# Retention with two mixtures: signs of weight conversions on ScalarE, sums and splits at other queue places

## The chip, the cores and the metric

The kernel runs on one core of a Trainium2 chip. Its time is the device time of one execution in microseconds (us), and the median of several executions is compared. Five engines work side by side, each through its own queue, in order: TensorE (PE in the profile, its weight loads PEld), VectorE (DVE), ScalarE (ACT), GpSimd (POOL) and SyncE (SP, here only issuing DMA transfers). An instruction waits at the head of its queue until what it needs is there, and everything behind it waits too.

## The reference

Three stages follow one another. First a retention layer over two sequences of 768 tokens and 8 heads of 64, in blocks of 64 tokens with a state that is carried on and decays by `lam` per head:

```python
intra = np.einsum('bhij,bhjd->bhid', np.einsum('bhic,bhjc->bhij', qb, kb) * Dmask[None], vb)
inter = np.einsum('bhid,bhde->bhie', qb * lam_pow[None], kv_state)
out[:, :, sl] = intra + inter
kv_state = lam_block[None, :, None, None] * kv_state + np.einsum('bhsd,bhse->bhde', kb_dec, vb)
```

Its output, 1536 tokens by 512, goes through a layer with 2048 hidden units, `relu(x @ w_in)**2 @ w_out`, and then through one with 1536 hidden units:

```python
gate = 1.0 / (1.0 + np.exp(-(x @ w_gate)))
val = x @ w_val
return (gate * val @ w_out).astype(np.float32)
```

The weights of both layers arrive in float64; `w_gate` is large (scaled by 45.7).

## The kernel before

**Weights.** The program reads a weight unit (128 x 512 numbers) as pairs of 32-bit words (`raw`) and makes fp32 from the bits. There are 68 such conversions: 32 units of the first layer (`w1`) and 36 of the second (`w2`: gate, val and output unit for each of 12 blocks of 128 hidden units). `conv_act` is the part on ScalarE: `j` from the high words (L155), and `r` from the low words. It has two forms. With `sign=False`, `r` is one operation (L163). With `sign=True`, ScalarE writes `r` in two 16-bit halves: the lower from the low words (L159), the upper, with sign, from the high words (L161). `conv_dve` is the part on VectorE: a shift of `j` (L186, or L196 for the units whose sign is turned over), then L189, which merges the sign, and the addition (L181). With `sign=True` L189 is left out. Before the change 16 conversions, all in the first layer, use that form. The result is stored in DRAM and read back when it is used.

**Splits.** Every fp32 matrix enters TensorE as a sum of a high part (cast to fp32r on ScalarE: `whi`, `xch`, `ah`, `gh`, `gq`, `wq`) and a low part (difference on VectorE: `wlo`, `xcl`, `al`, `gl`). Each product is three matmuls: high by high, high by low, low by high. The names in the profile are these tiles, `p` is a PSUM bank.

**The second layer.** From 311 to 407 us TensorE works on the first 512 tokens, block by block (`step_2`): `stage_a` (L472) makes gate and val of block f, `stage_b` (L486) the output part of block f-1. In between, `elem` makes `g` (sigmoid `r` on ScalarE at L507, product on VectorE at L508) and `split_g` makes `gh` (L516) and `gl` (L518). For block f+1, `split_w` makes three `whi` (L458) and three `wlo` (L460). The other 1024 tokens go by Strassen's scheme: `combine_x` prepares the seven token combinations (`t` at L577 and L583, casts `xch` at L561, `xcl` at L564) while the first 512 tokens are in work. From 407 to 527 us `strassen` multiplies with the gate and val weights, a key (two blocks, gate or val) after the other; per key seven products A11, S1, S2, S4, S3, A12, A22 (`block`, L678). `snap` copies a bank to SBUF on ScalarE (`s`, L687) before a later product may add into the bank; `total` (`c`, L692) adds on VectorE. Gate results go through the sigmoid at L792, val results are multiplied with it (L796). Then `later` makes the four sums `gs` (L813), which with `g` are the seven operands of the output product; `by_unit` splits them into `gq` high (L859) and low (L862). From 527 us to the end `blocks_out` (L995) multiplies them with seven combinations of output weights, in two passes q of the six blocks. The weight combinations `ws` come from `sum_out_w` (four VectorE operations at L924 for each of six block pairs, one load `wr` before and four stores after). `prepare_w` loads them (`bring`, into the two places D and `rows` in turn), casts `wq` (L948) and subtracts (L952).

**What sets the order.** All of it is recorded by one program that walks along TensorE's instructions with a model clock. `at(pos, fn)` puts work on an agenda; when `passed` moves the clock past `pos`, the agenda's `fn` is recorded there, on whichever engines it uses. `T3`, `T4`, `T5` and `T6` are model times at which the second layer, its Strassen part, the output passes and the second of these begin. The queue order of each engine is thus fixed when the program is built, and the times in the agenda are model times, not measured ones.

Of the kernel before, what the change touches and what calls it, by code (L numbers as in the profile page):

```python
# [7 lines left out]
F32 = mybir.dt.float32  # L8
F32R = mybir.dt.float32r
AF = mybir.ActivationFunctionType  # L10
# [28 lines left out]
def retention_moe_kernel(  # L39
# [24 lines left out]
    nc = tc.nc  # L64
# [25 lines left out]
    clock = [0.0]  # L90
    agenda = []

    def at(pos, fn):
        agenda.append((pos, len(agenda), fn))
# [47 lines left out]

    ready = []

    def conv_act(more=True, sign=False):

        if not to_conv or to_conv[0] not in raw_t:
            return  # L150
        key = to_conv.pop(0)
        t = raw_t.pop(key)
        j = unit("j")
        r = unit("r", I32)
        nc.scalar.activation(j, t[:, :, 1].bitcast(F32), AF.Copy, scale=2.0**-112)  # L155
        low = t[:, :, 0].bitcast(mybir.dt.uint32)
        if sign:
            parts = r.bitcast(mybir.dt.int16).rearrange("p (n two) -> p n two", two=2)
            nc.scalar.activation(parts[:, :, 0], low, AF.Copy, scale=2.0**-29)  # L159
            top = parts[:, :, 1].bitcast(mybir.dt.float16)  # L160
            nc.scalar.activation(top, t[:, :, 1].bitcast(F32), AF.Copy, scale=2.0**-60)  # L161
        else:
            nc.scalar.activation(r, low, AF.Copy, scale=2.0**-29)  # L163
        ready.append((key, j.bitcast(I32), r, sign))
        if more:
            load_w(1)

    def conv_dve():

        if not ready:  # L170
            return []
        key, j, r, sign = ready.pop(0)
        ph, f, u = key
        flip = ph == 2 and u < 2 and f % 2 == 0
        m = unit("m", I32)
        w = unit("u")
        if ph == 1:
            w_t[key] = w

        def last():  # L180
            nc.vector.tensor_tensor(out=w.bitcast(I32), in0=m, in1=r, op=ALU.add)  # L181
            n_stored[0] += 1
            at(clock[0] + 4.0, lambda: nc.sync.dma_start(out=w32[ph][f, u], in_=w))

        ops = [
            lambda: nc.vector.tensor_scalar(  # L186
                out=m, in0=j, scalar1=3, scalar2=None, op0=ALU.logical_shift_left
            ),
            lambda: nc.vector.scalar_tensor_tensor(  # L189
                out=m, in0=j, scalar=-(2**31), in1=m, op0=ALU.bitwise_and,  # L190
                op1=ALU.bitwise_xor if flip else ALU.bitwise_or,
            ),
            last,
        ]
        if flip:
            ops[0] = lambda: nc.vector.tensor_scalar(  # L196
                out=m, in0=j, scalar1=3, scalar2=-(2**31),
                op0=ALU.logical_shift_left, op1=ALU.bitwise_or,
            )
        if sign:  # L200
            assert not flip
            ops.pop(1)
        return ops

# [582 lines left out]
    def pair_in_2(i):  # L787
        gate = {}

        def use_gate(di, t, c, in_psum):  # L790
            r = gate[di, t] = unit("r")
            nc.scalar.activation(r, c, AF.Sigmoid)  # L792

        def use_val(di, t, c, in_psum):
            g = unit("g")
            nc.vector.tensor_tensor(out=g, in0=c, in1=gate.pop((di, t)), op=ALU.mult)  # L796
            n = GB.get((di, t))
            raw[n] = g
            if n is not None:
                done(n)  # L800
            if n == 5:
                later()

        raw = {}

        def done(n):
            if i in VIA_DRAM:
                g = raw[n]
                at(clock[0] + 2.5, lambda: nc.sync.dma_start(out=gs_dram[i, :, n], in_=g))

        def total(n, a, b, op):
            raw[n] = unit("gs")
            nc.vector.tensor_tensor(out=raw[n], in0=raw[a], in1=raw[b], op=op)  # L813
            done(n)

        def later():


            t = clock[0] + (7.5 if i == 5 else 0.0)
            at(t + 1.5, lambda: total(0, None, 6, ALU.add))  # L820
            at(t + 3.5, lambda: total(1, 0, 4, ALU.subtract))
            at(t + 5.5, lambda: total(2, 4, None, ALU.subtract))
            at(t + 7.5, lambda: total(3, 5, 1, ALU.subtract))
            if i in VIA_DRAM:
                at(t + 7.5, raw.clear)
            elif i == 0:
                at(t + 7.5, lambda: by_unit(i, dict(raw), clock[0], 4.5))
            else:
                at(t + 7.5, lambda: by_unit(i, dict(raw), T5 + 16.5, 0.8))

        return [use_gate, use_val]
# [22 lines left out]
    def by_unit(i, raw, pos, gap):  # L854

        def hi(n):
            if i not in gq:
                new_set(i)
            nc.scalar.copy(block_of(gq[i][0], n), raw[n])  # L859

        def lo(n):
            nc.vector.tensor_tensor(  # L862
                out=block_of(gq[i][1], n), in0=raw.pop(n), in1=block_of(gq[i][0], n),
                op=ALU.subtract,
            )

        for k, n in enumerate((4, 5, 1, 0, 2, 3, 6)):
            at(pos + gap * k, lambda n=n: hi(n))
            at(pos + gap * k + 1.2, lambda n=n: lo(n))
# [96 lines left out]
    def blocks_out():  # L966


        for q in range(2):
            acc, v = {}, {}  # L970

            def put(name, t, e, cols=slice(0, TB), eng=nc.sync):
                col = (t + 1) * TB
                eng.dma_start(
                    out=out[2 * q + e, :, col + cols.start : col + cols.stop],
                    in_=v[name][:, cols],
                )

            def add(name, k, other, cols=slice(0, TB)):
                if name not in v:  # L980
# [162 lines left out]
        stage_b(*prev.pop())  # L1143
        evacuate(ph)

    def convert(pos):
        at(pos, conv_act)
        at(pos + 2.0, lambda: run(conv_dve()))


# [2 lines left out]
    T3 = T2 + 24 * NF1 * MM  # L1153
    T4 = T3 + (36 * NF2 - 12) * MM
    T5 = T4 + (12 + 42 * NF2) * MM

    with tc.manual_schedule():
# [95 lines left out]
        for f in range(2, NF2):  # L1253
            at(T3 + (36 * (f - 1) - 12) * MM - 8.0, lambda f=f: load_units(2, f))
        for k in range(3 * NF2 - n_out):
            convert(T3 + 2.0 + 3.6 * k)
        for i in range(NF2 // 2):
            sum_out_w(i, T4 - 64.0 + 9.0 * i)
        keys = [(2, i, u) for i in range(NF2 // 2) for u in range(2)]
        prepare_a(keys[0], T4)  # L1260
        at(T4 - 28.0, lambda: combine_a((2, 0, 1)))
# [2 lines left out]
        for f in range(NF2):  # L1264
            step_2(f)
        T6 = T5 + 6 * STEP
        by_unit_through_dram(1, T5 - 14.0, T5 - 7.0)
        through_dram(2, T5 - 4.0, T5 + 1.5)
        through_dram(3, T5 + 1.0, T5 + 6.5)
        through_dram(4, T5 + 6.0, T5 + 11.5)  # L1270
        for n, load, pos in (
            (0, -21.0, -13.0), (1, -12.0, -1.5), (2, -6.0, 4.0),
            (3, 1.0, 8.8), (4, 6.0, 13.5), (5, 11.0, 18.3),
        ):
            prepare_w(0, n, n, T5 + load, T5 + pos)
        for n, i, load, pos in (
            (0, 5, -12.5, -5.0), (1, 4, -7.5, -1.0), (2, 3, -3.0, 3.5),
            (3, 0, 1.0, 8.0), (4, 2, 6.0, 12.5), (5, 1, 10.0, 15.5),
        ):
            prepare_w(1, n, i, T6 + load, T6 + pos)  # L1280
        by_unit_through_dram(2, T6 - 7.0, T6 + 5.0)
# [68 lines left out]
```

## Time and profile before

| | us |
|---|---|
| runs, lowest, median, highest | 589.77, 589.95, 595.18 |
| profiled execution | 591.19 |
| its span in the trace | 589.4 |
| PE busy | 576.1 (98%) |
| DVE busy | 474.0 (80%) |
| ACT busy | 366.9 (62%) |

The span is the time from the first to the last instruction in the trace of one execution, and the execution's own time is 1.8 us longer. Busy time is the time in which an engine worked on at least one instruction. TensorE's granted clock is 1.00 of its full rate in all stretches shown. Records of matmuls overlap: a new one may start every 0.227 us, and the record of one lasts 0.39. In the timelines a number in brackets is the idle time just before an instruction, and behind the arrow stands what ended it.

### The profile page before, as it was taken

The numbers are of one execution on the slowest core, as the hardware profiler recorded it, in microseconds if no ns is written. First come the engines' busy times: TensorE is split into PE (matmuls) and PEld (weight loads), VectorE is DVE, ScalarE is ACT, GpSimd is POOL, SyncE is SP. The second block draws the span as 40 slices with busy tenths as digits, with TensorE's granted clock in tenths as the row PEclk, the third lists the DMA queues.
The fourth block names the chain that finished last, engine by engine and source line by source line (L and its number), as shares of the span: only waits on it lengthen the run. The fifth ranks groups of instructions, "written<-read, shape, count | busy, mean of one in ns | idle before, by whom it ended". The sixth has DMA issues, their size and how long they took to land.

```text
span 589.4 us, 9045 instructions
## 1 busy us (share of the span) xinstructions
PE 576.1 (98%) x3172; PEld 471.7 (80%) x3172; DVE 474.0 (80%) x732; ACT 366.9 (62%) x605; POOL 47.6 (8%) x48
## 2 busy tenths in 40 slices
PE   9899999999999999999999999999999999999996
PEld 8788888767888888888888887888887888878885
DVE  2789896899788868988777788985678877789974
ACT  4679999997656557756467645544545554475470
POOL 1751100000000000000000000022012110000000
PEclk9999999999999999999999999999999999999999
DMA  7999896783253297999978878994547678488681
GB/s 260 413 405 376 311 310 216 226 293 105 71 189 134 108 304 263 413 408 413 404 273 289 307 246 272 339 305 102 174 89 205 187 229 233 153 320 307 205 304 72
DMA packets 69008, 150.83 MB, mean 256 GB/s; under 512 B 7137, under 2 KB 14305, under 8 KB 68962
## 3 DMA queue, kind: packets, MB, share of 16 engines
q1 hardware_dynamic: 64656, 144.34, 68.8%
q0 software_dynamic: 3360, 3.93, 4.5%
q10 hardware_dynamic: 946, 1.97, 1.0%
q8 instruction: 25, 0.41, 0.3%
q14 instruction: 21, 0.17, 0.1%
HBM read 106.43 MB, written 42.21 MB: 252 GB/s over the span
## 4 chain that ended last, share of the span: by engine, by line
PE 80%; DVE 9%; ACT 4%; DMA 3%; issue 3%; POOL 0%; DVEq 0%; SPq 0%; ACTq 0%
PE p L678 28%; PE p L1066 15%; PE p L472 15%; PE p L486 10%; PE p L995 8%; DMA gr<-gs 2%; PE p L315 2%; PE p L400 2%; DMA decay<-w_dram 1%; DVE at L350 1%; PE p L383 1%; DVE m L189 1%; PE p L411 1%; DVE gq L862 1%; DVE xcl L564 1%
## 5 line engine op out<-in xcount | busy, mean ns | idle before, releaser
L678 PE MATMUL p<-xch,ah 128*128 128x512 f32 x280 | 110.0, 393 | 1.0 <-ACT s L687 0.5
L678 PE MATMUL p<-xcl,ah 128*128 128x512 f32 x280 | 109.1, 390 | 0.0
L678 PE MATMUL p<-xch,al 128*128 128x512 f32 x280 | 109.1, 390 | 0.0
L678 PEld LDWEIGHTS p<-xch,ah 128*128 128x128 f32 x280 | 52.6, 188 | 15.3 <-ACT s L687 3.5
L687 ACT COPY s<-p 128x512 f32<-128x512 f32 x60 | 35.2, 588 | 43.8 <-PE p L678 43.7
L678 PEld LDWEIGHTS p<-xch,al 128*128 128x128 f32 x280 | 52.6, 188 | 11.0
L678 PEld LDWEIGHTS p<-xcl,ah 128*128 128x128 f32 x280 | 52.6, 188 | 10.6
L995 PE MATMUL p<-gq,wq 128*128 128x512 f32 x252 | 57.7, 390 | 1.0 <-DVE wq L952 1.0
L692 DVE TENSOR_TENSOR c<-p,s 128x512 f32<-128x512 f32 x60 | 41.2, 687 | 19.4 <-PE p L678 19.0
L995 PEld LDWEIGHTS p<-gq,wq 128*128 128x128 f32 x252 | 47.2, 188 | 11.4 <-DVE wq L952 1.6
L155 ACT ACTIVATE j<-raw 128x512 f32<-128x512 f32 x68 | 45.7, 672 | 12.9 <-issue 5.3
L181 DVE CUSTOM_DVE_ANT_0 u<-m,r 128x1024 uint16<-128x1024 uint16 x68 | 49.6, 729 | 4.7 <-ACT r L161 1.7
L460 DVE TENSOR_TENSOR wlo<-u,whi 128x512 fp32r<-128x512 f32 x68 | 46.0, 708 | 6.2 <-ACT whi L458 5.0
L1066 PE MATMUL p<-g2h,whi 128*128 128x512 f32 x128 | 49.8, 389 | 0.0
L1066 PE MATMUL p<-g2l,whi 128*128 128x512 f32 x128 | 49.8, 389 | 0.0
L1066 PE MATMUL p<-g2h,wlo 128*128 128x512 f32 x128 | 49.8, 389 | 0.0
L472 PE MATMUL p<-xh,wlo 128*128 128x512 f32 x160 | 43.8, 395 | 3.8 <-DVE wlo L460 3.8
L472 PE MATMUL p<-xh,whi 128*128 128x512 f32 x160 | 43.2, 392 | 0.0
L472 PE MATMUL p<-xl,whi 128*128 128x512 f32 x160 | 42.8, 390 | 0.0
L163 ACT ACTIVATE r<-raw 128x512 int32<-128x512 uint32 x52 | 34.5, 663 | 8.2 <-PE p L1066 4.9
L472 PEld LDWEIGHTS p<-xh,wlo 128*128 128x128 f32 x160 | 29.4, 188 | 12.6 <-DVE wlo L460 6.9
L458 ACT CAST whi<-u 128x512 fp32r<-128x512 f32 x68 | 37.9, 615 | 0.5 <-PE p L472 0.5
(129 smaller groups left out, 1048.3 us busy)
## 6 DMA issues: line engine op xcount, KB each, us to landing
raw<-in_w SPq DMA_DIRECT2D x68, 512.0 KB, 6.4
w<-u SPq DMA_DIRECT2D x68, 256.0 KB, 5.1
u<-w SPq DMA_DIRECT2D x52, 256.0 KB, 5.1
a<-w SPq DMA_DIRECT2D x20, 512.0 KB, 4.1
g<-g SPq DMA_DIRECT2D x32, 256.0 KB, 4.4
g<-g SPq DMA_DIRECT2D x16, 512.0 KB, 7.6
gr<-gs SPq DMA_DIRECT2D x24, 256.0 KB, 5.6
kv<-in_kv SPq DMA_DIRECT2D x11, 512.0 KB, 10.4
```

The costliest lines, as they stand in the source:

```text
L155: nc.scalar.activation(j, t[:, :, 1].bitcast(F32), AF.Copy, scale=2.0**-112)
L163: nc.scalar.activation(r, low, AF.Copy, scale=2.0**-29)
L181: nc.vector.tensor_tensor(out=w.bitcast(I32), in0=m, in1=r, op=ALU.add)
L458: nc.scalar.copy(hi, src)
L460: lambda lo=lo, src=src, hi=hi: nc.vector.tensor_tensor(out=lo, in0=src, in1=hi, op=ALU.subtract)
L472: nc.tensor.matmul(acc, lhsT=a[:, kk * P : (kk + 1) * P], rhs=b[:, kk, :], start=i == 0, stop=i == 11,)
L486: nc.tensor.matmul(acc[e], lhsT=a[:, e * P : (e + 1) * P], rhs=b, start=first and i == 0, stop=last and i == 2,)
L678: nc.tensor.matmul(acc, lhsT=w[:, col, kk * P : (kk + 1) * P], rhs=x[:, kk, :], start=start and i == 0, stop=stop and i == 5, skip_group_c ...
L687: nc.scalar.copy(s, acc)
L692: nc.vector.tensor_tensor(out=c, in0=acc, in1=s, op=ALU.add)
L995: nc.tensor.matmul(acc[k], lhsT=a[:, wn], rhs=block_of(b, gn), start=first and n == 0, stop=last and n == 3 * len(group) - 1,)
L1066: nc.tensor.matmul(acc[e, t], lhsT=a[:, e * P : (e + 1) * P], rhs=b[:, t, :], start=first and i == 0, stop=last and i == 2,)
```

## The change

Four things change; the arithmetic does not, and TensorE's and GpSimd's instructions stand in the same order as before.

- The 12 conversions recorded in the second layer use `sign=True`, so that ScalarE does L159 and L161 for L163, and VectorE leaves out L189. `flipped` tells which units turn their sign over; for these the scale of L161 is negative.
- `sum_out_w` stands 12 us later on the agenda.
- The splits of the operands of the output product move: `by_unit(0)` has a step of 5.5 for 4.5, `by_unit_through_dram(1)` and `through_dram(2)` begin 1 to 2 us earlier. Some `prepare_w` of both passes move by 0.5 to 2.5 us.
- The stores of the first output pass are recorded 2 us later by the model clock, all of them on SyncE; one was on ScalarE.

```diff
--- before.py
+++ after.py
@@ -141,6 +141,9 @@
             raw_t[key] = t
 
     ready = []
+
+    def flipped(key):
+        return key[0] == 2 and key[2] < 2 and key[1] % 2 == 0
 
     def conv_act(more=True, sign=False):
 
@@ -158,7 +161,8 @@
             parts = r.bitcast(mybir.dt.int16).rearrange("p (n two) -> p n two", two=2)
             nc.scalar.activation(parts[:, :, 0], low, AF.Copy, scale=2.0**-29)
             top = parts[:, :, 1].bitcast(mybir.dt.float16)
-            nc.scalar.activation(top, t[:, :, 1].bitcast(F32), AF.Copy, scale=2.0**-60)
+            sg = -1.0 if flipped(key) else 1.0
+            nc.scalar.activation(top, t[:, :, 1].bitcast(F32), AF.Copy, scale=sg * 2.0**-60)
         else:
             nc.scalar.activation(r, low, AF.Copy, scale=2.0**-29)
         ready.append((key, j.bitcast(I32), r, sign))
@@ -171,7 +175,7 @@
             return []
         key, j, r, sign = ready.pop(0)
         ph, f, u = key
-        flip = ph == 2 and u < 2 and f % 2 == 0
+        flip = flipped(key)
         m = unit("m", I32)
         w = unit("u")
         if ph == 1:
@@ -192,13 +196,12 @@
             ),
             last,
         ]
-        if flip:
+        if flip and not sign:
             ops[0] = lambda: nc.vector.tensor_scalar(
                 out=m, in0=j, scalar1=3, scalar2=-(2**31),
                 op0=ALU.logical_shift_left, op1=ALU.bitwise_or,
             )
         if sign:
-            assert not flip
             ops.pop(1)
         return ops
 
@@ -824,7 +827,7 @@
             if i in VIA_DRAM:
                 at(t + 7.5, raw.clear)
             elif i == 0:
-                at(t + 7.5, lambda: by_unit(i, dict(raw), clock[0], 4.5))
+                at(t + 7.5, lambda: by_unit(i, dict(raw), clock[0], 5.5))
             else:
                 at(t + 7.5, lambda: by_unit(i, dict(raw), T5 + 16.5, 0.8))
 
@@ -971,10 +974,12 @@
 
             def put(name, t, e, cols=slice(0, TB), eng=nc.sync):
                 col = (t + 1) * TB
-                eng.dma_start(
-                    out=out[2 * q + e, :, col + cols.start : col + cols.stop],
-                    in_=v[name][:, cols],
-                )
+                dst = out[2 * q + e, :, col + cols.start : col + cols.stop]
+                c = v[name][:, cols]
+                if q == 0:
+                    at(clock[0] + 2.0, lambda: nc.sync.dma_start(out=dst, in_=c))
+                else:
+                    eng.dma_start(out=dst, in_=c)
 
             def add(name, k, other, cols=slice(0, TB)):
                 if name not in v:
@@ -1143,8 +1148,8 @@
         stage_b(*prev.pop())
         evacuate(ph)
 
-    def convert(pos):
-        at(pos, conv_act)
+    def convert(pos, sign=False):
+        at(pos, lambda: conv_act(True, sign))
         at(pos + 2.0, lambda: run(conv_dve()))
 
 
@@ -1253,9 +1258,9 @@
         for f in range(2, NF2):
             at(T3 + (36 * (f - 1) - 12) * MM - 8.0, lambda f=f: load_units(2, f))
         for k in range(3 * NF2 - n_out):
-            convert(T3 + 2.0 + 3.6 * k)
+            convert(T3 + 2.0 + 3.6 * k, True)
         for i in range(NF2 // 2):
-            sum_out_w(i, T4 - 64.0 + 9.0 * i)
+            sum_out_w(i, T4 - 52.0 + 9.0 * i)
         keys = [(2, i, u) for i in range(NF2 // 2) for u in range(2)]
         prepare_a(keys[0], T4)
         at(T4 - 28.0, lambda: combine_a((2, 0, 1)))
@@ -1264,18 +1269,18 @@
         for f in range(NF2):
             step_2(f)
         T6 = T5 + 6 * STEP
-        by_unit_through_dram(1, T5 - 14.0, T5 - 7.0)
-        through_dram(2, T5 - 4.0, T5 + 1.5)
+        by_unit_through_dram(1, T5 - 16.0, T5 - 8.5)
+        through_dram(2, T5 - 5.0, T5 + 1.5)
         through_dram(3, T5 + 1.0, T5 + 6.5)
         through_dram(4, T5 + 6.0, T5 + 11.5)
         for n, load, pos in (
-            (0, -21.0, -13.0), (1, -12.0, -1.5), (2, -6.0, 4.0),
+            (0, -21.0, -13.0), (1, -12.0, -0.5), (2, -6.0, 4.0),
             (3, 1.0, 8.8), (4, 6.0, 13.5), (5, 11.0, 18.3),
         ):
             prepare_w(0, n, n, T5 + load, T5 + pos)
         for n, i, load, pos in (
-            (0, 5, -12.5, -5.0), (1, 4, -7.5, -1.0), (2, 3, -3.0, 3.5),
-            (3, 0, 1.0, 8.0), (4, 2, 6.0, 12.5), (5, 1, 10.0, 15.5),
+            (0, 5, -12.5, -5.0), (1, 4, -7.5, -1.0), (2, 3, -3.0, 2.5),
+            (3, 0, 0.5, 6.0), (4, 2, 6.0, 10.0), (5, 1, 8.0, 13.0),
         ):
             prepare_w(1, n, i, T6 + load, T6 + pos)
         by_unit_through_dram(2, T6 - 7.0, T6 + 5.0)
```

Line numbers behind L144 are larger by 3 to 5 in the changed kernel. Three places show how the queues change.

The first is VectorE's queue in the middle of the second layer's first 512 tokens, at the token combination `t`. `ws` are the sums of output weights, `wlo` the low parts of the next block's weights. Before:

```order
L564 TENSOR_TENSOR xcl<-xr_2718,xch 128x1024
L577 TENSOR_TENSOR t<-xr_2718,xr_2719 128x1024
L924 TENSOR_TENSOR ws<-wr 128x2x128
L924 TENSOR_TENSOR ws<-wr,ws 128x2x128
L924 TENSOR_TENSOR ws<-wr 128x2x128
L924 TENSOR_TENSOR ws<-wr,ws 128x2x128
L460 TENSOR_TENSOR wlo<-u,whi 128x512 x3
L564 TENSOR_TENSOR xcl<-t,xch 128x1024
```

After:

```order
L567 TENSOR_TENSOR xcl<-xr_2718,xch 128x1024
L580 TENSOR_TENSOR t<-xr_2718,xr_2719 128x1024
L463 TENSOR_TENSOR wlo<-u,whi 128x512 x3
L567 TENSOR_TENSOR xcl<-t,xch 128x1024
L927 TENSOR_TENSOR ws<-wr 128x2x128
L927 TENSOR_TENSOR ws<-wr,ws 128x2x128
L927 TENSOR_TENSOR ws<-wr 128x2x128
L927 TENSOR_TENSOR ws<-wr,ws 128x2x128
```

The sum that stood between `t` and `wlo` is no longer there; a sum now stands behind the next `xcl`. The same happens at the next `t` (L583, now L586).

The second is VectorE's queue in the second Strassen stage, in the pair of keys near 457 us of the profile. `c` is a sum of two products, `al` the low part of the next key's weights, `as` their Strassen sums. Before:

```order
L692 TENSOR_TENSOR c<-p,s 128x512
L657 TENSOR_TENSOR al<-as,ah 128x1024
L692 TENSOR_TENSOR c<-p,s 128x512
L813 TENSOR_TENSOR gs<-g 128x512
L813 TENSOR_TENSOR gs<-g,gs 128x512
L692 TENSOR_TENSOR c<-p,s 128x512
L637 TENSOR_TENSOR as<-a 128x256
L638 TENSOR_TENSOR as<-a 128x256
L639 TENSOR_TENSOR as<-as,a 128x256
L640 TENSOR_TENSOR as<-a,as 128x256
L862 TENSOR_TENSOR gq<-gs,gq 128x512
L657 TENSOR_TENSOR al<-a,ah 128x768
```

After:

```order
L695 TENSOR_TENSOR c<-p,s 128x512
L660 TENSOR_TENSOR al<-as,ah 128x1024
L695 TENSOR_TENSOR c<-p,s 128x512
L816 TENSOR_TENSOR gs<-g 128x512
L865 TENSOR_TENSOR gq<-gs,gq 128x512
L816 TENSOR_TENSOR gs<-g,gs 128x512
L695 TENSOR_TENSOR c<-p,s 128x512
L640 TENSOR_TENSOR as<-a 128x256
```

The `gq` that stood behind the four `as` now stands between the two `gs`, ahead of the last `c`.

The third is ScalarE's queue in the last key of that stage, near 519 us. `s` is the copy of a bank, `r` a sigmoid, `gq` the cast of an operand of the output product, `gr` what is read back from DRAM for it. Before:

```order
L792 ACTIVATE r<-c 128x512 x2
L687 COPY s<-p 128x512
L792 ACTIVATE r<-p 128x512
L859 CAST gq<-gr 128x512
L687 COPY s<-p 128x512
L859 CAST gq<-gr 128x512
L687 COPY s<-p 128x512
L859 CAST gq<-gr 128x512 x4
```

After:

```order
L795 ACTIVATE r<-c 128x512 x2
L690 COPY s<-p 128x512
L862 CAST gq<-gr 128x512
L795 ACTIVATE r<-p 128x512
L862 CAST gq<-gr 128x512 x2
L690 COPY s<-p 128x512
L862 CAST gq<-gr 128x512
L690 COPY s<-p 128x512
L862 CAST gq<-gr 128x512 x2
```

Ahead of the second `s` shown there are now three casts `gq` where one stood.

## Rows read from the trace of the kernel before

**Rows 1.** The page's busy line: busy us (share of the span) and instructions of each engine.

```profile
PE 576.1 (98%) x3172; PEld 471.7 (80%) x3172; DVE 474.0 (80%) x732; ACT 366.9 (62%) x605; POOL 47.6 (8%) x48
```

**Rows 2.** Waits of PE, 340 to 590 us: engine, line, releaser: us, times, longest.

```profile
PE p L995 <- DVE wq L952: 1.0, 1, 1.0
```

**Rows 3.** Stretches: length, busy PE PEld DVE ACT POOL, clock, DMA share, GB/s.

```profile
344.00:360.00 16.00, 15.52 (x68) 12.27 (x67) 14.15 (x28) 7.71 (x14) 0.00 (x0) 1.00 0.78 249
360.00:407.00 47.00, 47.00 (x209) 38.90 (x208) 39.78 (x63) 24.03 (x38) 6.18 (x6) 1.00 0.92 281
```

**Rows 4.** Groups of instructions: busy us, mean ns | idle before, releasers.

```profile
L189 DVE SCALAR_TENSOR_TENSOR m<-j,m 128x512 int32<-128x512 int32 x52 | 35.9, 690 | 1.2
L163 ACT ACTIVATE r<-raw 128x512 int32<-128x512 uint32 x52 | 34.5, 663 | 8.2 <-PE p L1066 4.9 <-PE p L486 2.9 <-PE p L472 0.3
L159 ACT ACTIVATE r<-raw 128x512 int16<-128x512 uint32 x16 | 12.6, 786 | 0.2 <-PE p L486 0.2
L161 ACT ACTIVATE r<-raw 128x512 f16<-128x512 f32 x16 | 12.4, 772 | 0.0
```

**Rows 5.** Timeline near 359: start, duration, instruction [idle before <-releaser].

```profile
359.15 1.21 PE L472 MATMUL p<-xh,wlo 128*128 128x512 f32 x4 [0.48 <-DVE wlo L460]
```

**Rows 6.** Timeline 347 to 363, ACT and DVE.

```profile
347.64 1.65 ACT L458 CAST whi<-u 128x512 fp32r<-128x512 f32 x3
349.48 1.89 DVE L460 TENSOR_TENSOR wlo<-u,whi 128x512 fp32r<-128x512 f32 x3
361.58 0.69 DVE L518 TENSOR_TENSOR gl<-g,gh 128x512 fp32r<-128x512 f32 x1 [0.69 <-ACT gh L516]
362.40 1.66 ACT L458 CAST whi<-u 128x512 fp32r<-128x512 f32 x3
```

**Rows 7.** Timeline 370 to 400, DVE and PE.

```profile
370.85 0.41 DVE L924 TENSOR_TENSOR ws<-wr 128x256 f32<-128x256 f32 x1
372.57 1.90 DVE L460 TENSOR_TENSOR wlo<-u,whi 128x512 fp32r<-128x512 f32 x3 [0.17 <-ACT whi L458]
398.26 1.89 DVE L460 TENSOR_TENSOR wlo<-u,whi 128x512 fp32r<-128x512 f32 x3 [1.64 <-ACT whi L458]
399.21 1.07 PE L472 MATMUL p<-xh,whi 128*128 128x512 f32 x4
```

**Rows 8.** Timeline 457 to 463, ACT, DVE and PE.

```profile
457.72 0.60 ACT L859 CAST gq<-gs 128x512 fp32r<-128x512 f32 x1
458.27 0.68 DVE L692 TENSOR_TENSOR c<-p,s 128x512 f32<-128x512 f32 x1
460.25 0.58 ACT L687 COPY s<-p 128x512 f32<-128x512 f32 x1
461.25 0.39 PE L678 MATMUL p<-xch,ah 128*128 128x512 f32 x1
462.14 0.60 ACT L687 COPY s<-p 128x512 f32<-128x512 f32 x1
462.79 0.50 PE L678 MATMUL p<-xch,ah 128*128 128x512 f32 x1
```

**Rows 9.** Timeline near 480, ACT and PE.

```profile
479.65 0.57 ACT L687 COPY s<-p 128x512 f32<-128x512 f32 x1
480.61 0.39 PE L678 MATMUL p<-xch,ah 128*128 128x512 f32 x1
```

**Rows 10.** Timeline 519 to 521, ACT and PE.

```profile
519.60 0.62 ACT L859 CAST gq<-gr 128x512 fp32r<-128x512 f32 x1
520.11 0.60 ACT L687 COPY s<-p 128x512 f32<-128x512 f32 x1
520.78 0.48 PE L678 MATMUL p<-xch,ah 128*128 128x512 f32 x1
```

**Rows 11.** Timeline 571 to 578, ACT and PE.

```profile
571.28 0.94 ACT L948 CAST wq<-D 128x896 fp32r<-128x896 f32 x1 [0.29 <-DMA D<-wt]
577.06 1.20 PE L995 MATMUL p<-gq,wq 128*128 128x512 f32 x4 [1.00 <-DVE wq L952]
```


## The prediction

> **What bounds the kernel now.** I read the busy line first, then the list of TensorE's waits, then a table by stretches, and then the timelines around each wait. TensorE (PE) is busy 98% of the span [rows 1], so there is little left to win: the change touches nothing before the second layer (from 311 us), and the waits that the list names from 340 us to the end are short; the longest is 1.0 us, on a subtraction for the output weights [rows 2]. TensorE's instructions and their order are the same in both kernels, so the time changes only by what TensorE waits. Just before 360 us VectorE (DVE) is the fullest helper, busy 14.15 of 16 us, while ScalarE (ACT) has 7.71 [rows 3]. That is where the moved signs act; the moved sums act behind it.
>
> In what follows a matmul's slot is 0.227 us (two of them in a row start that far apart), its record lasts 0.39, and one that had to wait records 0.50 [rows 8], so each stop costs about 0.11 us beside the wait.
>
> **The change, part by part.**
>
> *Signs.* Each of the twelve conversions loses the VectorE operation L189, 0.69 us, and has the two ScalarE operations L159 and L161 (0.786 and 0.772) where L163 (0.663) stood [rows 4]. Operations that follow one another on ScalarE overlap by about 0.10 (a cast of 0.62 [rows 10], three of them 1.65 [rows 6]), so a conversion costs ScalarE 0.786 + 0.772 - 0.663 - 0.10 = 0.80 more. Twelve times: VectorE -8.3 us, ScalarE +9.6.
> The gain is bounded by what TensorE waits there. At 359.15 it stood idle 0.48 for a `wlo` [rows 5]; the record before runs 0.16 past its slot, and the stop costs 0.11: 0.75 us. Two L189 lie between that `wlo` and the one before, so it will be 1.4 us earlier, and this wait goes: **-0.75**.
> What limits the `wlo` ahead of it is now ScalarE: the cast `whi` at 347.64 comes 0.69 earlier (its chain starts behind a VectorE conversion) but has two longer conversions before it, +1.60. So it starts at 348.55, its first third ends at 349.17, and `wlo` starts at 349.21 in place of 349.48 [rows 6]: VectorE gains only 0.27 here.
>
> *Output-weight sums.* This is the largest term. A sum is four operations that take 1.55 us, 370.85 to 372.40 [rows 7]. In two units of this layer a sum stood in VectorE's queue behind `t`, where VectorE otherwise waits for two ScalarE casts (`xch`, then `whi`) until `wlo` may start: 370.85 to 372.57 is 1.72 us, of which the sum filled all but 0.17 [rows 7]. After the change the queue has `t` and `wlo` next to one another there, and the sums elsewhere, where nothing is waited for. I follow VectorE in three steps to the last unit.
> From the `wlo` of 349.48 to that of 372.57: two L189 gone, -1.38; before, three sums and the rest of 0.17, now two sums and one empty place of 1.72, together 0; and a new stop of 0.87, since the `wlo` that began at 363.65 now follows `gl` directly (its end 362.19) and needs a `whi` that is ready at 362.40 + 0.62 + 0.04 = 363.06 [rows 6]. Together -0.51.
> From there to the last `wlo` (398.26): before, two sums and 0.17; now three sums and one empty place. 3 x 1.55 + 1.72 - 2 x 1.55 - 0.17 = +3.10.
> So the last unit's `whi` and `wlo` come 3.10 - 0.51 - 0.27 = 2.32 us later, since `t` on VectorE releases the casts. The first cast is ready at about 400.58 where TensorE, 0.75 early, would begin at 399.21 - 0.75 = 398.46 [rows 7]: a **new wait of 2.1 us**. Ends: 1.4 if the cast conversions overlap ScalarE's idle time and the 0.87 stop doesn't arise, 2.9 if VectorE is not earlier at 349.48 at all and an `xcl` (1.2) comes in front; I take the worked value, which rests on neighbouring rows alone.
> The sixth sum now lies behind the layer's last units, where VectorE has room; its cover is the whole first key of the second Strassen stage, and without it it would cost its 1.55. With each sum one load and four stores move 12 us later on SyncE, so that the weight loads of the units and the first loads of the Strassen stage pass them; the transfers' share of 360 to 407 us is 0.92 [rows 3], and what leaves that stretch can only help those that stay. I cost that at 0; if a load is late nevertheless, the 0.29 that the last pass waits for one [rows 11] is the nearest row.
>
> *Splits in the second Strassen stage.* The gap of by_unit(0), 5.5 for 4.5, moves the VectorE half of a split (`gq` lo, 0.60 from start to start) to later queue places.
> At the pair of keys near 457 it goes from behind the sums `as` to between two `gs`. There it also waits for its own cast, begun at 457.72 and done at 458.32. So `c`, at 458.27 before, comes at 458.36 + 0.60 + 0.61 = 459.57, 1.30 later [rows 8]. `c` releases a sigmoid on ScalarE, and the bank copies `s` stand behind that sigmoid in its queue: the copy that began at 460.25 ends at 462.13 instead of 460.83. TensorE needs its bank at 461.25: wait 0.94 with the signal's 0.05, plus 0.11, **+1.05**. The second copy (462.14 + 0.60 + 1.31 = 464.05) is then needed at 462.62 + 1.05 = 463.67: 0.43 + 0.11, against 0.17 + 0.11 now, **+0.26** [rows 8].
> At the next such pair one `gq` (0.60) comes in between: the copy at 479.65 ends at 480.82 for a matmul that starts at 480.61 [rows 9]: 0.26 + 0.11, **+0.37**, and its second wait grows like the one above, **+0.25**.
> At the last key it is by_unit_through_dram(1), placed 1.5 us earlier: two more of its `gq` casts, 0.51 each from start to start, now stand in ScalarE's queue before the copy of 520.11, which ends at 521.73, and the matmul of 520.78 has waited only 0.09 so far [rows 10]: 1.00 + 0.11 - 0.09, **+1.02**. A cast here delays the copies that free TensorE's banks; ScalarE's share of 62% [rows 1] hides that.
>
> *The last pass.* The wait at 577.06 (1.0 in the list, 1.27 from slot to slot) is for the last `wq` lo; it follows a `wq` whose cast began at 571.28 behind its transfer, 0.29 late [rows 2, 11], and whose lo came behind splits. Fewer splits stand ahead of it now (7 instead of 10 of this pass). If the transfer lands where it does, that gives 0.29; if the pass also starts 1.0 earlier beside TensorE, because the casts that cost the last key its 1.02 are already done, all 1.27. The second follows from my own term, so I take **-1.27** and keep -0.29 as the other end.
>
> *Stores.* Three of the first pass's four stores already went out by SyncE; the fourth moves there, and all come 2 us later by the program's clock. On SyncE they stand between loads that must be in order, but the number of transfers ahead of the decisive load stays the same, and ScalarE waits there anyhow: 0. The ends, -0.3 and +0.3, are taken from the 0.29 that the cast at 571.28 waited for its transfer [rows 11].
>
> **Sum:** -0.75 + 2.12 + 1.05 + 0.26 + 0.37 + 0.25 + 1.02 - 1.27 = **+3.05 us**. The profiled execution took 591.19 (span 589.4); it would be 594.2. The median of the runs, 589.95, is 1.24 below it, so the median after is about **593.0**.
>
> What the conversions cost may be weighed against a page. The trace has 0.786 and 0.772 for the two operations that write 16-bit halves [rows 4]. The Trainium skill (ScalarE: Activation LUTs, section What ACT_TABLE_LOAD costs) gives one price for an ACTIVATE with immediate scale, 186 ns + 0.833 ns for each element, whatever the type, and an overlap of 93 ns; that makes 613 ns here, and a conversion would cost ScalarE 0.52 more, the `wlo` would start 0.56 earlier again, the wait of 2.1 would be 1.6 and the sum +2.5 by this estimate. The rows speak against one price for all outputs, and the sum goes by them.
>
> **The rivals.**
> 1. *VectorE catches up* (0.20). The 2.1 wait doesn't arise, because other idle time of VectorE takes up the empty places. For it: ahead of the `wlo` of 398.26 VectorE waited 1.64 for its cast [rows 7]. Against: the `t` that releases the cast stands in VectorE's own queue, behind all that is moved. Then 3.05 - 2.12 = +0.93: 590.9.
> 2. *All new waits are absorbed* (0.17): the copies have more room than I give them and only the gains are left, -0.75 - 1.27 = -2.0: 587.9. For it: the helpers are at 80% and 62% on the average [rows 1]; against it, the matmul at 462.79 already records 0.50 [rows 8], so the slack at this place is nil.
> 3. *Slower by over 1%* (0.07): the longer conversions lie on the chain of the units. Each `g` goes from VectorE to ScalarE for `gh` and back for `gl`; where a conversion stands directly ahead of a `gh`, its 0.80 comes on top of that way, and the L189 that is saved lies behind it, where VectorE waits anyhow. If TensorE has no slack in the unit it waits 0.80 each time. With 5.9 - 3.05 = 2.85 to go, four of the twelve are enough; with six it is 3.05 + 4.8 = 7.9: 597.8. Against it: ScalarE idles 8.3 of 16 us there [rows 3]. The Trainium skill's advice to give additions and multiplications to VectorE, not to ScalarE (ScalarE: Activation LUTs, section Rules for kernel authors), is of this kind; no run here shows yet which engine such work suits at this place.
> 4. *Nothing moves* (0.03): the order lists show that instructions do move, so this would need every new wait to cancel: 589.95.
>
> My forecast has 0.53; its own range is 591.5 to 594.7, from the ends 1.4 and 2.9 of the large wait and -0.29 of the last pass, less 0.5 where one Strassen wait fails to come. To hold 8 in 10 the range takes in rival 1 and the middle of rival 2: 587.9 to 595.2. A measurement of this kernel can tell 1%, 5.9 us, from no change: faster by more would need over the 2.0 us of gains that exist, 0.01; slower by more is rival 3 and a little of the forecast's tail, 0.08; within 1%: 0.91.
>
> **What would show it.** In the changed kernel: VectorE's L189 gone from the second layer and its busy time some 8 us lower, ScalarE's some 9 higher; no wait near 359; a wait of about 2 us on `whi` or `wlo` at the first matmuls of the last unit, near 399; waits of 1 us on `s` near 461 and 521; and none near 577. If the wait near 399 is missing while the empty place stands behind `t`, the largest step is wrong; if the waits near 461 and 521 are missing, the copies had room that I overlooked.

## The result, and the profile after

The changed kernel is slower by 0.6%: median 594.80 us of 19 executions, against 590.96 of 19 of the kernel before; ratio 1.0061 (1.0050 to 1.0073). The profiled execution took 596.51, its span 594.7. It is one of five in which the mean granted clock was 0.997 or less; those five have a median of 595.63, the other fourteen 594.46. Three of the fourteen took 595.39 to 595.61 at a clock of 1.00, so the clock does not explain the whole spread.

The forecast of 593.0 was counted from the three runs known before, with a median of 589.95. Of the 1.8 us that it lacks, 1.0 is that kernel's own median, 590.96 over nineteen executions; the rest is the difference, 3.84 for the forecast 3.05. The measured 594.80 lies just above the forecast's own range (591.5 to 594.7) and inside the wide one (587.9 to 595.2).

The busy line of the changed kernel answers to [rows 1]:

```profile
PE 578.3 (97%) x3172; PEld 472.5 (79%) x3172; DVE 465.6 (78%) x722; ACT 373.5 (63%) x615; POOL 48.3 (8%) x48
```

VectorE is 8.4 us less busy (forecast 8.3), ScalarE 6.6 more busy (forecast 9.6). The moved operations show in the groups by form; L193, L167, L162 and L165 are now what L189, L163, L159 and L161 are in [rows 4]:

```profile
L193 DVE SCALAR_TENSOR_TENSOR m<-j,m 128x512 int32<-128x512 int32 x42 | 28.9, 688 | 0.9
L167 ACT ACTIVATE r<-raw 128x512 int32<-128x512 uint32 x42 | 27.9, 665 | 4.9 <-PE p L1071 4.8
L162 ACT ACTIVATE r<-raw 128x512 int16<-128x512 uint32 x26 | 20.3, 782 | 0.4 <-PE p L489 0.4
L165 ACT ACTIVATE r<-raw 128x512 f16<-128x512 f32 x26 | 20.0, 768 | 0.0
```

Ten conversions, not twelve, took the new form: L167 and L193 each have ten operations fewer than in [rows 4], L162 and L165 ten more. Of VectorE's 8.4 us that is 6.9.

TensorE's waits from 340 us to the end (engine, line, releaser: us in total, times, longest), to be read against [rows 2]:

```profile
PE p L681 <- ACT s L690: 2.7, 5, 0.8
PE p L475 <- ACT whi L461: 1.9, 1, 1.9
PE p L681 <- DVE c L695: 0.4, 1, 0.4
PE p L1000 <- DVE wq L955: 0.4, 1, 0.4
```

No wait for `wlo` is left: the one of 359.15 [rows 5] is gone. A wait for `whi` has come, and the waits for `s` went from one of 0.5 to five. The wait for `whi` is the last unit's, and the timeline shows how it arises (start, duration, instruction, idle time before and what ended it):

```profile
369.04 1.22 DVE L580 TENSOR_TENSOR t<-xr,xr 128x1024 f32<-128x1024 f32 x1
371.89 1.90 DVE L463 TENSOR_TENSOR wlo<-u,whi 128x512 fp32r<-128x512 f32 x3 [1.64 <-ACT whi L461]
397.66 1.22 DVE L586 SCALAR_TENSOR_TENSOR t<-t,xr 128x1024 f32<-128x1024 f32 x1
398.91 1.04 ACT L564 CAST xch<-t 128x1024 fp32r<-128x1024 f32 x1 [5.22 <-DVE t L586]
399.86 1.66 ACT L461 CAST whi<-u 128x512 fp32r<-128x512 f32 x3
400.52 1.25 PE L475 MATMUL p<-xh,whi 128*128 128x512 f32 x4 [1.95 <-ACT whi L461]
401.58 1.91 PE L475 MATMUL p<-xh,wlo 128*128 128x512 f32 x4
403.28 1.85 PE L475 MATMUL p<-xl,whi 128*128 128x512 f32 x4
404.98 1.08 PE L475 MATMUL p<-xh,whi 128*128 128x512 f32 x4
```

In the kernel before, the `t` of the last unit was here:

```profile
395.41 1.22 DVE L583 SCALAR_TENSOR_TENSOR t<-t,xr 128x1024 f32<-128x1024 f32 x1
```

The place behind the first `t` is empty now: VectorE stands 1.64 us where a sum stood in [rows 7]. The `t` of the last unit comes at 397.66, 2.25 later than before, its casts follow at once, and TensorE starts at 400.52: 2.11 late, and 0.11 for the stop. Then something follows that the forecast did not have. Four matmuls take 1.07 us in a record of [rows 7]; here the second and third four take 1.91 and 1.85. The stretches say why (length, busy time of the five engines, granted clock, transfers' share, GB/s):

```profile
398.00:400.40 2.40, 0.57 (x3) 0.15 (x1) 0.87 (x1) 1.49 (x3) 0.00 (x0) 1.00 0.70 226
400.40:401.60 1.20, 1.08 (x5) 0.88 (x6) 1.10 (x2) 1.20 (x4) 0.00 (x0) 0.97 0.00 0
401.60:405.20 3.60, 3.60 (x10) 2.81 (x9) 3.40 (x5) 0.57 (x2) 0.00 (x0) 0.53 0.02 7
405.20:410.00 4.80, 4.80 (x23) 3.95 (x22) 3.86 (x7) 2.28 (x4) 0.00 (x0) 1.00 0.19 73
```

About 1.0 us after TensorE started again the granted clock fell to its lower level, 1.2 of 2.4 GHz (0.53 over the stretch). Eight matmuls started 0.43 apart instead of 0.23: 1.6 us. At 405 us the clock was back.

The Strassen stage near 461 of before is this (all the stops before it have moved it by 3 us):

```profile
461.44 0.69 DVE L865 TENSOR_TENSOR gq<-gs,gq 128x512 fp32r<-128x512 f32 x1 [0.61 <-ACT gq L862]
462.65 0.68 DVE L695 TENSOR_TENSOR c<-p,s 128x512 f32<-128x512 f32 x1
463.37 0.63 ACT L795 ACTIVATE r<-c 128x512 f32<-128x512 f32 x1 [1.96 <-DVE c L695]
464.63 0.58 ACT L690 COPY s<-p 128x512 f32<-128x512 f32 x1
465.26 0.50 PE L681 MATMUL p<-xch,ah 128*128 128x512 f32 x1 [0.76 <-ACT s L690]
467.18 0.50 PE L681 MATMUL p<-xch,ah 128*128 128x512 f32 x1 [0.27 <-ACT s L690]
```

It is the forecast chain, link by link: the split waits 0.61 for its cast, `c` is late, the sigmoid `r` is late, and the copy `s` behind it stops TensorE. [Rows 8] are its counterpart. At the last key three casts stand ahead of the copy, where [rows 10] had one; the last two of them:

```profile
525.01 1.14 ACT L862 CAST gq<-gr 128x512 fp32r<-128x512 f32 x2
526.04 0.59 ACT L690 COPY s<-p 128x512 f32<-128x512 f32 x1
526.69 0.50 PE L681 MATMUL p<-xch,ah 128*128 128x512 f32 x1 [0.85 <-ACT s L690]
```

In the last pass the `wq` whose cast had waited 0.29 for its transfer [rows 11] now waits 3.96, and the stop behind it is shorter:

```profile
576.75 0.94 ACT L951 CAST wq<-D 128x896 fp32r<-128x896 f32 x1 [3.96 <-DMA D<-wt]
582.28 1.90 PE L1000 MATMUL p<-gq,wq 128*128 128x512 f32 x7 [0.40 <-DVE wq L955]
```

### The profile page after: what moved, and what is told of

It is laid out like the page before. It is cut to its first block, busy times and chain, and to the rows that moved or that the text cites. A ratio compares the mean times of both kernels' runs of the same rounds, so it can differ in the third digit from the quotient of the medians.

```text
span 594.7 us, 9048 instructions
## 1 busy us (share of the span) xinstructions
PE 578.3 (97%) x3172; PEld 472.5 (79%) x3172; DVE 465.6 (78%) x722; ACT 373.5 (63%) x615; POOL 48.3 (8%) x48
## 4 chain that ended last, share of the span: by engine, by line
PE 71%; DVE 12%; DMA 6%; ACT 6%; issue 4%; SPq 0%; POOL 0%; DVEq 0%; ACTq 0%
PE p L681 27%; PE p L1071 15%; PE p L475 10%; PE p L489 8%; PE p L1000 6%; PE p L318 2%; DVE wlo L463 2%; PE p L403 2%; DMA wt<-ws 1%; DVE xcl L567 1%; DMA decay<-w_dram 1%; DVE at L353 1%; DMA gr<-gs 1%; DVE ws L927 1%; DMA D<-wt 1%
## 5 line engine op out<-in xcount | busy, mean ns | idle before, releaser
L185 DVE CUSTOM_DVE_ANT_0 u<-m,r 128x1024 uint16<-128x1024 uint16 x68 | 48.2, 708 | 5.0 <-ACT r L165 2.1
L475 PEld LDWEIGHTS p<-xh,whi 128*128 128x128 f32 x160 | 29.9, 189 | 8.9 <-ACT whi L461 2.4
```

Of the source, the lines that this page charges most:

```text
L475: nc.tensor.matmul(acc, lhsT=a[:, kk * P : (kk + 1) * P], rhs=b[:, kk, :], start=i == 0, stop=i == 11,)
```

## The experiments

Below, a stop is what TensorE lost, from slot to slot: the wait and the 0.11. Sizes of stops come from one profiled execution of each kernel, two for the changed one and for the sums alone.

**Signs alone.** The kernel before, with only this and the `flipped` code that it needs:

```diff
-            convert(T3 + 2.0 + 3.6 * k)
+            convert(T3 + 2.0 + 3.6 * k, True)
```

> The kernel before with the signs on ScalarE alone; sums, splits, last-pass loads and stores stand where they stood. Theory (the moved sums make the stop near 400 us, the signs alone only save): the stops near 350 and 359 (0.18 + 0.75) go, no new one appears, the one near 577 (1.27) stays; 0.93 us less than before, ratio 0.9984, VectorE some 8 us less busy. Rival (the longer conversions on ScalarE delay whi and gh): a stop of 1 us or more near 399, and no gain, ratio 1.001 or more.

Measured: 590.14, ratio 0.9993 (0.9979 to 1.0007). The waits of TensorE from 340 us on:

```profile
PE p L997 <- DVE wq L955: 0.8, 1, 0.8
PE p L681 <- ACT s L690: 0.5, 1, 0.5
PE p L681 <- DVE c L695: 0.4, 1, 0.4
```

Neither a wait for `wlo` nor one for `whi`. The signs do not make the stop near 400, and the two stops before 360 are gone. Whether that shows as time (0.9984 lies inside the interval, and so does 1) these runs don't decide.

**Sums back.** The changed kernel with `sum_out_w(i, T4 - 64.0 + 9.0 * i)` again.

> The changed kernel with the output-weight sums back at their old places. Theory: the stop near 400 (2.22) is gone, and with it the stretch of low granted clock behind it (8 matmuls 0.43 apart, 1.6 us in the profile of the changed kernel); the stops of the Strassen stage stay (2.8 more than before), the last pass keeps its gain of 0.6. Against before: -0.93 + 2.84 - 0.6 = +1.3, ratio 1.0022. Rival (the signs make the stop): a stop near 400 stays, ratio 1.004 or more. Rival on the clock (it falls without regard to the stop): granted clock under 1.00 near 400 still.

Measured: 592.08, ratio 1.0016 (1.0002 to 1.0030). No stop near 400, the clock full there. The Strassen stops repeat (1.03 and 0.55, 0.32 and 0.54, 1.12). The last pass did not keep its gain: its stops add up to 1.45. So the moved sums cost 0.45% of the 0.61%, with all that changes behind them.

**Splits back.** The changed kernel with the gap of `by_unit(0)` and `by_unit_through_dram(1, T5 - 14.0, T5 - 7.0)` as before.

> The changed kernel with the two moved splits (gap of by_unit(0), begin of by_unit_through_dram(1)) back at their old places. Theory: the stops near 465, 467, 485, 487 and 527 go back to before's sizes, 2.84 us less than the changed kernel; the stop near 400 and the low clock behind it stay. Of the last pass two readings: as the prediction had it, its gain hangs on the casts done earlier, then its wait is back near 1.2; or it comes from the moved loads, then it stays near 0.6 or falls. Against before: -0.93 + 2.2 + 1.6 (where the clock falls) - 0.6 = +2.3, ratio 1.0039; without the fall +0.7. Rival (the stops come from elsewhere, such as later loads): they stay, ratio as the changed kernel's.

Measured: 593.36, ratio 1.0039 (1.0025 to 1.0054). That is the ratio expected with the low clock, but not by the expected terms: the last pass lost 0.30 where a gain of 0.6 was expected, and in the profile the clock did not fall behind the stop; six of eleven executions have a mean clock of 0.997 or less. Its waits:

```profile
PE p L475 <- ACT whi L461: 2.0, 1, 2.0
PE p L1000 <- DVE wq L955: 0.9, 1, 0.9
PE p L681 <- ACT s L690: 0.5, 1, 0.5
PE p L681 <- DVE c L695: 0.4, 1, 0.4
```

The four new waits for `s` are gone: they belong to the splits. The last pass stops for 1.64 in all, as in the first of the two readings. That the earlier casts make the difference to 0.67 is not shown: the clock fell near 400 in the profile with 0.67 and not in this one, and the filled kernel below has the earlier casts and stops 1.59.

**Sums alone.** The kernel before with only `sum_out_w` 12 later; run twice.

> The kernel before with the moved sums alone, signs and splits as before. Theory: a stop of about 2 us near 399, since the places behind t are empty as in the changed kernel and no L189 is saved; the granted clock may fall behind it as there (1.6 us). The stops near 350 and 359 (0.93) get smaller, as fewer sums stand ahead. Against before: +1.5 to +2, or +3 to +3.6 with the fall of the clock; ratio 1.003 to 1.006. Rival (stop made by the longer conversions): no stop near 399, ratio 1.000.

> The kernel with the moved sums alone once more, on the same chip as the one with the small matmuls, for comparison. Theory: about two thirds of the executions at 0.997 or less, median 593.8. Rival (the share of low executions goes with the chip or the hour, not with the stop): a share like that of the kernel before.

Measured: ratio 1.0045 (1.0029 to 1.0060) and 1.0049 (1.0037 to 1.0061). The stop in the first of them:

```profile
400.82 1.20 PE L472 MATMUL p<-xh,whi 128*128 128x512 f32 x4 [2.40 <-ACT whi L458]
```

It is 2.67 us (2.59 in the second), longer than with the signs, where L189 is saved, and in neither profile did the clock fall behind it. So the sums alone make the stop, without any moved sign.

**Stop filled.** Small matmuls in the stop, in the changed kernel and in the kernel with the sums alone:

```diff
             accs.append(bank())
+            if (ph, f, u) == (2, NF2 - 1, 0):
+                for _ in range(40):
+                    nc.tensor.matmul(accs[u][:, 0:P], lhsT=warm, rhs=warm, start=True, stop=True)
```

> The changed kernel with 40 small matmuls (128 x 128 by 128 columns, into the bank that the last unit overwrites) on TensorE just ahead of the last unit's first products, so that TensorE works through the stop near 400 us instead of standing idle. Theory (standing idle for over 2 us is what makes the clock fall in some executions): the stop itself costs the same 2.2, but the executions with a granted clock of 0.997 or less become as rare as in the kernel before (4 of 34) instead of about half (18 of the 41 of the three kernels with the stop). Median 0.3 to 1 us below the changed kernel, ratio to before 1.005 to 1.006. Rival (the fall has nothing to do with standing idle there): as many low executions as with the stop, ratio as the changed kernel's, 1.006.

> The kernel with the moved sums alone (stop of 2.67 us near 400, granted clock of 0.997 or less in 8 of 11 executions), with 48 small matmuls on TensorE in that stop. Theory (the clock falls in many executions because TensorE stands idle there): no more than 2 or 3 of 12 executions at 0.997 or less, and a median about 0.5 us lower than the same kernel without the small matmuls. Rival (the falls come from elsewhere): as many as without them.

Measured: ratios 1.0072 (1.0056 to 1.0089) and 1.0057 (1.0040 to 1.0074), no better than unfilled (1.0061 and 1.0049). By the medians the second, six executions, is 0.71 lower than the same kernel unfilled on the same chip, five executions (593.11, 593.82), so whether filling helps these runs don't decide. In the profile of the first, TensorE works through the stop:

```profile
399.52 2.41 PE L501 MATMUL p<-warm 128*128 128x128 bf16 x40
```

and the stretch behind it has the full clock (columns as above):

```profile
401.00:405.00 4.00, 4.00 (x31) 3.44 (x29) 3.39 (x5) 2.11 (x5) 0.00 (x0) 1.00 0.03 6
```

The three unfilled profiles of the kernels with splits back and with the sums alone have the full clock there too, so this proves little. And that execution had its low clock at the very start, 0.97 and 0.96 in the first two stretches to 43 us, before any of this. Counted by execution, the mean clock was 0.997 or less in 21 of 46 with the idle stop (5 of 19, 6 of 11, 7 of 11 where the expectation says 8, 3 of 5), in 3 of 12 with the filled one, in 9 of 63 of the kernel before, and in 7 of 41 of the other kernels without the stop. More executions are low with the idle stop than without it; the filled ones are too few to say that standing idle is the reason. In the last pass the first of the two filled kernels, which has all the edits, stops for 0.43 and 1.16, 1.59 in all:

```profile
PE p L1003 <- DVE wq L958: 0.9, 1, 0.9
PE p L1003 <- ACT wq L954: 0.2, 1, 0.2
```

**Last pass alone.** The changed kernel with sums and splits back: signs, and the loads, casts and stores of the output passes.

> The changed kernel with sums and splits at their old places: what is left is the signs and the moved loads, casts and stores of the output passes. The prediction had a gain of 1.27 in the last pass; the profile of the changed kernel has 0.6, the two experiments with sums or splits back have none (waits there add up to 1.45 and 1.64, against 1.34 before). Theory now: these edits gain nothing by themselves; the stops of the last pass add up to 1.1 to 1.6, the time is that of the signs alone, ratio 0.9984 to 0.9993. Rival (the edits do gain, and the other moves hide it): under 0.7 of stops, ratio 0.998 or less.

> One more profile of the kernel with the signs and the moved loads, casts and stores of the output passes, sums and splits at their old places. Theory (these edits gain nothing in the last pass): stops there add up to 1.1 to 1.6, no stop near 359 nor near 400; the Strassen stops as in the kernel before. Rival: under 0.7 there.

Measured: 590.55, ratio 0.9995 (0.9983 to 1.0007); like the signs alone. The profile has more than expected:

```profile
PE p L1000 <- DVE wq L955: 0.9, 1, 0.9
PE p L1000 <- ACT wq L951: 0.9, 1, 0.9
PE p L681 <- ACT s L690: 0.5, 1, 0.5
PE p L681 <- DVE c L695: 0.4, 1, 0.4
```

The stops of the last pass are 0.30, 1.13 and 1.17: 2.60, against 1.34 before. In this profile the edits by themselves make the last pass worse; the time does not show it.

**The change once more,** unaltered, for a second profile.

> One more profile of the changed kernel, unaltered. Theory: the stops near 400 (2.22) and of the Strassen stage repeat within 0.05; the 0.67 of the last pass does not repeat, since it hangs on when transfers land (1.0 to 1.6 here), and the stretch behind the stop may have the full clock this time. Rival: 0.67 again, then the last pass does gain 0.6 when all the edits stand together.

Measured: stop near 400 of 2.23, then eight matmuls 0.43 apart again; Strassen stops within 0.02 of the first profile's; the last pass 0.60. On the last pass the rival was right: it stopped for little again. But both these profiles have the clock's fall near 400, and the filled kernel, with all the edits and without that fall, stops 1.59; so the gain does not always come when all edits stand together.

**A better version.** The kernel before with the signs, the cast `ah` behind the copy instead of ahead of it, and the last reads 5 us earlier by the model clock. The line of the signs is left out here, and the two cuts are far apart in the kernel:

```diff
-            if nxt and not late:
-                high_a(nxt, 1)
             z = bank()
             block(z, key, S1, "T1", True, True)
             s5 = snap(z)
+            if nxt and not late:
+                high_a(nxt, 1)
...
-        by_unit_through_dram(2, T6 - 7.0, T6 + 5.0)
+        by_unit_through_dram(2, T6 - 12.0, T6 + 5.0)
```

> The kernel before with the signs on ScalarE and two other moves. In each Strassen key the cast ah of the next key's sums goes behind the copy s of the second product instead of ahead of it; and the reads of the last operand set (gr of block pair 2) are placed 5 us earlier, in front of a load that holds the SyncE queue for 5 us while no transfer runs. Theory (a cast ahead of a bank copy in ScalarE's queue is what stops TensorE at the fourth product): the stops of 0.19 in the first stage and 0.80, 0.29, 0.34 and 0.28 in the second go, 2.2 us together; the one near 577 goes too if the transfers are what is late, 1.27; with the signs' 0.93 the span is 4.4 us shorter, ratio 0.9926; without the last pass 0.9947. Rival (the stops come from the bank, not from the queue): they stay, ratio 0.998.

Measured: 587.09, ratio 0.9944 (0.9923 to 0.9965): faster than both kernels. ScalarE's queue in the key near 440, first in the kernel before, then here, and all that is left of TensorE's waits from 340 us on:

```profile
441.35 0.60 ACT L792 ACTIVATE r<-p 128x512 f32<-128x512 f32 x1
441.84 1.05 ACT L651 CAST ah<-as 128x1024 fp32r<-128x1024 f32 x1
442.77 1.08 ACT L687 COPY s<-p 128x512 f32<-128x512 f32 x2
```

```profile
440.11 0.58 ACT L690 COPY s<-p 128x512 f32<-128x512 f32 x1
440.57 1.07 ACT L654 CAST ah<-as 128x1024 fp32r<-128x1024 f32 x1
441.53 0.60 ACT L690 COPY s<-p 128x512 f32<-128x512 f32 x1
```

```profile
PE p L681 <- DVE c L695: 0.4, 1, 0.4
PE p L997 <- DVE wq L955: 0.4, 1, 0.4
```

The copy now stands ahead of the cast of 1.07, and no wait for `s` is named. One stop of 0.18 is left of the 0.80, 0.29, 0.34 and 0.28. At 573 us TensorE stops for 0.66 where the signs alone had 1.08: 0.4 less, not the 1.27 expected, and whether the earlier reads or the moved cast did it wasn't separated.

## Why the prediction came out

| step | forecast | first profile |
|---|---|---|
| stops before 360 | -0.75 | -0.93 |
| stop at the last unit | +2.12 | +2.22 |
| low clock behind it | not seen | +1.6 |
| Strassen, pair near 457 | +1.05, +0.26 | +1.03, +0.26 |
| Strassen, next pair | +0.37, +0.25 | +0.31, +0.20 |
| Strassen, last key | +1.02 | +1.04 |
| last pass | -1.27 | -0.67 |
| sum | +3.05 | +5.1 (3.5 without the clock) |

The profiled execution lost 2.0 us more than the sum: 1.6 for the clock and 0.6 for the last pass, with small differences of either sign beside them. That the median came nearer, 3.84, doesn't make these two terms right.

**Signs.** Right in what goes, a little small: it left out a stop of 0.18 at 350 (wait 0.07 and 0.11). `wlo` came at 349.04; the forecast had 349.21 by the rows. The two operations last what the rows said, 0.782 and 0.768, but they overlap by more than the 0.10 assumed: near 346 us they take 0.63 and 0.65 from start to start, where L163 took 0.57. So a conversion costs ScalarE about 0.71, not 0.80. The page's single price for an ACTIVATE (the Trainium skill, ScalarE: Activation LUTs, section What ACT_TABLE_LOAD costs), 613 ns at this size and stated for fp32 and bf16, does not fit outputs of 16-bit halves. The count was wrong too, ten for twelve; ten at 0.71 make 7.1, and ScalarE's busy time rose by 6.6. Neither total entered the sum, in which only the two conversions ahead of 347.64 and two L189 behind 349.48 stand.

**Sums.** The mechanism and the size were right, and the experiments confirm the cause: with the signs alone no stop, with the sums alone one of 2.67, with the sums back none. The three steps along VectorE's queue were forecast as -0.27, -0.51 and +3.10, 2.32 us later; they measured -0.44, -0.24 and +2.92, and `wlo` went from 398.26 to 400.50, 2.24. That the sum is within 0.08 is in part luck, since errors of up to 0.27 offset one another. The 2.12 is the wait alone; by the prediction's own rule 0.11 more belongs to such a stop, which makes 2.23 for the measured 2.22. The end of 1.4 did not come near. (The lower end of the forecast's own range, 591.5, is 591.8 by the terms it names.)

**The clock.** This is the term that the prediction didn't have. In both profiles of the changed kernel the granted clock fell behind the stop, and that cost 1.6; in the three profiles of the kernels with splits back and with the sums alone it did not fall. That the stop is the reason is likely by the counts above, not shown. The medians are 3.84 us apart, against 3.5 by the stops alone, so they may hold part of it; the interval of the ratio, 3.0 to 4.3 us, does not decide.

**Splits.** All five terms within 0.06.

**Last pass.** The sign was right and the size half, and a stop is left where the prediction wanted none. It put 0.29 on the edits and about 1.0 on the casts done earlier. The stops, one profile each, were 1.34 before, 2.60 with the edits, 1.45 with edits and splits moved, 1.64 with edits and sums moved, and with all 0.67 and 0.60, but 1.59 where the stop near 400 was filled. So the edits alone did not give their 0.29. That the casts gave 1.15 of it back fits the 2.60 and 1.45; it is not shown, because the pass waits for the `D` transfer, and this does not take the same time each time. From its issue on SyncE to the cast behind it, it took 5.7 and 5.5 us in the two profiles of the changed kernel and 7.0 in the filled one, which moves as much as the term itself. Besides, TensorE came 1.6 us later in those two by the low clock. The prediction had taken the landing as fixed. What makes it early or late stays open, so the half that came true is not shown to have come for the reason given.

**The rivals.** VectorE did not catch up, the new waits were not absorbed, and no unit waited for a conversion in front of `gh`: the third rival, the slower one, is excluded by the signs alone. The advice of the Trainium skill (ScalarE: Activation LUTs, section Rules for kernel authors) to use VectorE for such arithmetic did not decide here: with the operations on ScalarE both stops before 360 went.

## What to carry to other kernels

Follow one queue from the moved work to the next point at which the busiest engine needs it, and add up what fills a waiting place and what leaves it empty: four short operations behind `t` were free only as long as they stood where VectorE waited anyhow. In ScalarE's queue, put the copy that frees a bank ahead of casts that nobody waits for yet. And a part of a change that takes stops away can be hidden by a part that makes others: try the parts alone, and take more than one profile before you put a difference of half a microsecond behind a transfer down to an edit.

## What the runs showed of the hardware

TensorE's granted clock fell to 1.2 GHz for about 3.4 us, some 1.0 us after the end of a stop of 2.2 us, in both profiles of the changed kernel, and not behind stops of 2.25, 2.67 and 2.59 us in three profiles of two other kernels. In the kernel before, TensorE lost 1.9 us at 133 us and the clock stayed full. What distinguishes these cases stays open.

TensorE lost about 0.11 us beside the wait at each of these stops: the slot behind the first matmul was 0.34 us instead of 0.227.

On ScalarE, Copy at 128x512 took 0.782 and 0.768 us where it wrote every other 16 bits, and 0.665 where it wrote int32 from every other 32-bit word.
